# Reordering the prologue and the attention pace of a fused sparse-attention and softplus-MLP kernel

## The chip, the core and the metric

The kernel runs on one core of a Trainium2 chip. The metric is device time in microseconds of one execution; lower is better. A core has a matrix engine (TensorE, PE in the profile, with its weight loads listed as PEld), a vector engine (DVE), a scalar engine (ACT), GpSimd (POOL) and a queue processor that issues transfers (SyncE, SP). Matrix products land in PSUM; everything else on chip lives in SBUF.

## The reference

For 8 batches of 8 heads, 576 positions and head width 64, attention is computed with a mask: a position sees others at most 32 away, and 8 global positions see all and are seen by all. The result, 4608 tokens of width 512, goes through a two-layer product with a softplus between.

```python
scores = scale * np.matmul(q, k.transpose(0, 1, 3, 2))
mask = np.abs(pos[:, None] - pos[None, :]) <= window        # window = 32
mask = mask | is_global[:, None] | is_global[None, :]
scores = np.where(mask, scores, -1000000000.0)
attn = softmax(scores)
x = np.matmul(attn, v)                                       # heads side by side: 4608 x 512
h = x @ w_in                                                 # 512 x 2048
g = np.maximum(h, 0.0) + np.log1p(np.exp(-np.abs(h)))
out = g @ w_out                                              # 2048 x 512
```

## The kernel before

The work has two parts that share the engines: attention, batch by batch and in each batch by four pairs of heads, and the two-layer product, in 9 tiles of 512 tokens. Batch b fills columns 576b to 576b + 575 of `xT`, and tile n reads columns 512n to 512n + 511 of it, so tile 0 needs batch 0, tile 1 also batch 1, tile 2 also batch 2 and so on.

A pair of heads goes through these steps. `transposes` turns K and Q around on PE (line 258) into PSUM and copies them out to `KT` and `QT` (269, 271); the columns of the 8 global positions come from a one-hot product (263) in batches 0 and 1 and from `glob_T` through POOL copies (274 to 277) in later ones. `scores` multiplies them (291) and takes the exponential on ACT (299). `mask` multiplies with 0 or 1 on DVE (304). `sums` and `values` (325) multiply the result with ones and with V; `inv_ln` and `inv_exp` (344, 348) form the reciprocal of the sums on ACT; `scale_x` (357, 359) writes `xT` on DVE. `glob_sums` (335, 337) and `glob_norm` (365, 367) collect the rows of the global positions, and `glob_out` writes them into `xT` with 8 POOL copies (372).

A tile has 16 steps. In each, `mm1` makes one of 16 slices of the hidden layer (400: four 512-column matmuls into `hp`, then two ACT instructions, 403 and 404), and `mm2` does four of the 64 matmuls of the second product for the tile before (414); every fourth step ends with a copy of `o` (418) and a store. In tile 0 there is no `mm2`.

The order of the whole is written out by hand, and each engine runs its instructions in that order. Batch 0 is a prologue without tiles; its exponentials go into the buffer `first_ex`, and its global values come from a one-hot product (`value_globals`, 248). From then on `plan` holds, for each step and each of its two halves (after `mm1`, after `mm2`), the attention work to be done there. Times in the plan are counted in halves below: half 32 is the start of tile 1. `START` sets where batches 1 to 3 begin (steps 3, 20, 30, one pair each two steps); later batches have a pair each four steps, so that 16 steps hold a batch. `LOAD` and `CAST` set the step of a batch's loads and of its casts to bf16 on POOL.

Transfers of q, k, v and of the outputs are issued by SP in order (`load_runs` line 92, `load_v` 96). The weights are issued by POOL, cast on the way (`load_w_in` 424, `load_w_out` 428). The rows of K, Q and V at the global positions are gathered to a buffer in DRAM by `gather` (105) with 8 transfers per tensor, read back by `load_v_rows` (100) and by `load_global_columns` (380), cast (384) and transposed (388) into `glob_T`.

`warm` (502) runs matmuls on a constant tile whose result nobody reads. PSUM has in the prologue three two-bank regions for scores and value products (`region`) and two banks for transposes; later two regions, one transpose bank, two for `hp`, one for `o`.

Of the kernel before, what the change touches and what calls it, by code (L numbers as in the profile page):

```python
# [19 lines left out]
P = 128  # L20
# [20 lines left out]
def kernel(  # L41
# [42 lines left out]
    glob_T = {n: const.tile([P, NP, B * NG], BF16, name=f"{n}_gT") for n in "kq"}  # L84
    src = {"k": k, "q": q, "v": v}
    grow = {n: nc.dram_tensor(f"{n}_global_rows", (NG, B * HD), FP32, kind="Internal").ap() for n in "kqv"}
# [12 lines left out]
    def load_v_rows(b):  # L99
        nc.sync.dma_start(out=v_f[KW:P], in_=grow["v"][:, b * HD:(b + 1) * HD].unsqueeze(1).to_broadcast([NG, NTL, HD]))  # L100

    def gather(n, eng, first=0):
        sv = src[n].rearrange("b h s d -> (b h) s d")[first * H:]
        for g in range(NG):
            eng.dma_start(out=grow[n][g:g + 1, first * HD:].rearrange("o (c d) -> c o d", d=D),  # L105
                          in_=sv[:, bass.ds(regs[eng][g], 1), :])
# [22 lines left out]
    for p in range(2):  # L129
        load_runs("k", 0, [p])  # L130
        load_runs("q", 0, [p])
# [52 lines left out]
    load_v(0, half_heads[0])  # L184
    for p in range(2, NP):
        for n in "kq":
            load_runs(n, 0, [p])
    load_v(0, half_heads[1])
# [33 lines left out]
    masks = [const.tile([P, GW[i]], BF16, name=f"mask{i}") for i in range(2)]  # L222

    def scaled(eng, o, i, a, u=None):
        if eng is nc.scalar:
            eng.activation(out=o, in_=i, func=ACTF.Identity, scale=a, bias=0.0 if u is None else u)
        elif u is None:
            eng.tensor_scalar(out=o, in0=i, scalar1=a, scalar2=None, op0=ALU.mult)
        else:
            eng.tensor_scalar(out=o, in0=i, scalar1=a, scalar2=u, op0=ALU.mult, op1=ALU.add)  # L230

    def build_masks(tiles, eng):
        for t in tiles:
            m = masks[0 if t in GRP[0] else 1]
            c0 = GOFF[t] - (WLO[t] - (128 * t - 40))
            a, vl, n = akey[:, t:t + 1], vld[:, t:t + 1], ST[t]
            if t > 0:
                scaled(eng, m[:, c0:c0 + 40], band[:, 0:40], a)
            scaled(eng, m[:, c0 + 40:c0 + 40 + n], band[:, 40:40 + n], a, ukey[:])
            scaled(eng, m[:, c0 + 40 + n:c0 + 48 + n], band[:, 160:168], vl)  # L240
            if t < 4:
                scaled(eng, m[:, c0 + 168:c0 + 200], band[:, 168:200], a)
# [10 lines left out]
    def transposes(n, b, p, copy=nc.vector.tensor_copy):  # L253
        dst, rows = KT if n == "k" else QT, kqb[n, b]
        ps = psum["pool"].tile([P, 512], FP32, tag="tp", bufs=2 if b == 0 else 1, name="tp")
        tb = ps[:].bitcast(BF16)
        for r in range(RUN):
            nc.tensor.transpose(out=tb[:, r * NQ:(r + 1) * NQ], in_=rows[:, r, p * P:(p + 1) * P],  # L258
                                identity=ident_bf[:NQ, :NQ])
# [5 lines left out]
        else:  # L265
            copy = nc.vector.tensor_copy
            g = glob_T[n][:, p].rearrange("p (g b) -> p b g", b=B)[:, b]
# [17 lines left out]
    def scores(b, p, grp):  # L285
        sc = region(b, "sc")[:].rearrange("p (e c) -> p e c", e=2)
        for t in GRP[grp]:
            w = WHI[t] - WLO[t]
            for e in range(2):
# [3 lines left out]
                                 start=True, stop=True)  # L293
        if b == 0:
# [6 lines left out]

    def mask(p, grp):
        ex = exps[p, grp]
        nc.vector.tensor_tensor(out=ex, in0=ex, in1=masks[grp][:].unsqueeze(1).to_broadcast([P, 2, GW[grp]]),  # L304
# [10 lines left out]
    def over_keys(b, p, z, weights):  # L315
        av = AV[p, z] = region(b, "av")
        passes = [(slice(0, P), weights)]
        if b == 0 and not z:
            passes.append((slice(96, P), lambda t, e: VG[96:P, p * P + 64 * e:p * P + 64 * e + 64]))
        for j, (rows, weight) in enumerate(passes):  # L320
            for i, (t, lo, hi) in enumerate(PARTS):
                grp = 0 if t in GRP[0] else 1
                c = GOFF[t] + lo - WLO[t]
                for e in range(2):
                    nc.tensor.matmul(out=av[64 * e:64 * e + 64, OFF + lo:OFF + hi], lhsT=weight(t, e),  # L325
                                     rhs=exps[p, grp][rows, e, c:c + hi - lo],
                                     start=(j == 0 and lo in (0, SPLIT)),
                                     stop=(j == len(passes) - 1 and (i == len(PARTS) - 1 or hi == SPLIT)),
                                     skip_group_check=True, tile_position=(rows.start, 64 * e))
# [9 lines left out]
    def sums(b, p):  # L339
        over_keys(b, p, 1, lambda t, e: ones[:])  # L340
# [9 lines left out]
    def values(b, p):  # L350
        over_keys(b, p, 0, lambda t, e: V1[b % 2][:, t, p * P + 64 * e:p * P + 64 * e + 64])

    def scale_x(b, p):
# [5 lines left out]
        nc.vector.tensor_tensor(out=x[:, 480:576], in0=av[:, OFF + 512:OFF + 608], in1=rz[:, 512:608], op=ALU.mult)  # L359

# [14 lines left out]
    grows = {}  # L375

    def load_global_columns():
        for n in "kq":
            grows[n] = work.tile([B * NG, HD], FP32, tag=f"ex{0 if n == 'k' else 1}", bufs=2, name=f"{n}_rows")
            nc.sync.dma_start(out=grows[n][:], in_=grow[n].rearrange("g (b c) -> (g b) c", b=B))  # L380
# [232 lines left out]
```

## Time and profile before

| | us |
|---|---|
| median of 6 runs (386.74 to 388.4) | 387.56 |
| the profiled execution | 387.89 |
| its span, first to last instruction | 386.3 |
| PE busy | 347.3 (90%) |
| ACT busy | 275.4 (71%) |
| DVE busy | 182.6 (47%) |
| POOL busy | 119.2 (31%) |
| mean granted PE clock | 0.951 |
| moved by DMA | 43.64 MB, mean 113 GB/s |
| first `mm1` of tile 0 starts | 38.26 |
| first `mm1` of tile 1 starts | 74.94 |
| last `o` copy of tile 1 starts (step 15 of tile 2) | 164.85 |

Busy time is the time in which an engine has an instruction in work; for PE it also counts matmuls that run at a lowered clock, so it must be read together with the granted clock. A wait is written as the engine and line that waited, an arrow, and who released it, with the sum in us, the number of waits and the longest. A timeline has start, length, engine and line, the operation, output from inputs, the count, and in brackets the idle time before it with its releaser. The DMA share is the mean over 16 engines and can pass 1 where transfers overlap.

### The profile page before, as it was taken

The numbers are of one execution on the slowest core, as the hardware profiler recorded it, in microseconds if no ns is written. First come the engines' busy times: TensorE is split into PE (matmuls) and PEld (weight loads), VectorE is DVE, ScalarE is ACT, GpSimd is POOL, SyncE is SP. The second block draws the span as 40 slices with busy tenths as digits, with TensorE's granted clock in tenths as the row PEclk, the third lists the DMA queues.
The fourth block names the chain that finished last, engine by engine and source line by source line (L and its number), as shares of the span: only waits on it lengthen the run. The fifth ranks groups of instructions, "written<-read, shape, count | busy, mean of one in ns | idle before, by whom it ended". The sixth has DMA issues, their size and how long they took to land.

```text
span 386.3 us, 7411 instructions
## 1 busy us (share of the span) xinstructions
PE 347.3 (90%) x2761; PEld 178.1 (46%) x2801; DVE 182.6 (47%) x485; ACT 275.4 (71%) x438; POOL 119.2 (31%) x275
## 2 busy tenths in 40 slices
PE   6787877788888889999999999999999999999984
PEld 3564443334444444555455545554554444444432
DVE  7664177323665664675557556655554210100111
ACT  4742699764887787888888888888888767676500
POOL 7861770557308324343062308220200100000000
PEclk9556899996999999999999999999999999999999
DMA  7999449989519704591559156800000010010111
GB/s 168 240 260 212 100 76 214 252 199 235 105 39 235 160 30 139 162 143 45 151 151 160 55 152 158 152 28 29 29 27 30 27 56 27 27 56 27 53 57 54
DMA packets 62495, 43.64 MB, mean 113 GB/s; under 512 B 40932, under 2 KB 57444, under 8 KB 62460
## 3 DMA queue, kind: packets, MB, share of 16 engines
q1 hardware_dynamic: 57836, 38.86, 42.2%
q0 software_dynamic: 4480, 4.31, 6.8%
q8 instruction: 22, 0.36, 0.4%
q14 instruction: 13, 0.11, 0.1%
q10 hardware_dynamic: 144, 0.01, 0.0%
HBM read 37.92 MB, written 9.81 MB: 124 GB/s over the span
## 4 chain that ended last, share of the span: by engine, by line
PE 59%; issue 12%; DMA 9%; DVE 5%; SPq 5%; POOL 5%; ACT 1%; another core or an unknown queue 1%; POOLq 0%; ACTq 0%
PE o L414 27%; PE hp L400 22%; PE av L325 4%; PE tp L258 3%; PE sc L291 2%; SPq L105 2%; DVE ex L304 2%; DMA q_f<-in_q_dram 2%; DMA v_f<-in_v_dram 2%; POOL V L122 2%; DMA q_global_rows<-in_q_dram 2%; SPq L96 2%; DMA q_rows<-q_global_rows 1%; DMA v_f<-v_global_rows 1%
## 5 line engine op out<-in xcount | busy, mean ns | idle before, releaser
L400 PE MATMUL hp<-xT,w_in_t 128*128 128x512 bf16 x548 | 147.5, 385 | 3.7 <-POOL xT L372 2.1
L414 PE MATMUL o<-w_out_t,gt 128*128 128x512 bf16 x565 | 145.3, 381 | 4.4 <-DVE ot L418 3.3
L403 ACT ACTIVATE e<-hp 128x512 f32<-128x512 f32 x144 | 86.0, 597 | 61.0 <-PE hp L400 58.0
L404 ACT ACTIVATE gt<-e 128x512 bf16<-128x512 f32 x144 | 90.6, 630 | 4.5
L414 PEld LDWEIGHTS <-gt 128*128 128x128 bf16 x576 | 54.1, 98 | 67.5 <-issue 8.3
L400 PEld LDWEIGHTS <-w_in_t 128*128 128x128 bf16 x576 | 53.1, 99 | 65.9 <-issue 9.8
L418 DVE COPY ot<-o 128x512 f32<-128x512 f32 x36 | 24.8, 690 | 83.2 <-PE o L414 78.0
L304 DVE TENSOR_TENSOR ex<-ex,mask 128x1008 bf16<-128x1008 bf16 (+1 forms) x56 | 44.1, 795 | 30.7 <-ACT ex L299 29.7
L372 POOL COPY xT<-xg 128x4 bf16 x64 | 12.9, 202 | 129.7 <-DVE xg L367 126.3
L299 ACT ACTIVATE ex<-sc 128x1008 bf16<-128x1008 f32 (+1 forms) x56 | 48.5, 916 | 1.9 <-PE sc L291 1.9
L122 POOL CAST V<-v_f 128x512 bf16<-128x512 f32 (+3 forms) x50 | 27.8, 594 | 42.0 <-DMA v_f<-v_global_rows 36.3
L291 PE MATMUL sc<-QT,KT 64*128 64x200 bf16 (+2 forms) x320 | 21.5, 257 | 13.6 <-DVE xT L359 6.4
L344 ACT ACTIVATE rz<-av 128x616 f32<-128x616 f32 x32 | 21.8, 680 | 15.9 <-PE av L325 15.3
L269 DVE COPY KT<-tp 128x480 bf16<-128x480 bf16 x32 | 20.9, 652 | 25.7 <-PE tp L258 17.3
L118 POOL CAST qb<-q_f 96x1024 bf16<-96x1024 f32 (+1 forms) x24 | 24.3, 1031 | 7.5 <-DMA q_f<-in_q_dram 7.3
L118 POOL CAST kb<-k_f 96x1024 bf16<-96x1024 f32 (+1 forms) x24 | 24.5, 1044 | 3.9 <-PE sc L291 2.2
L335 DVE TENSOR_REDUCE gs<-av 128x8 f32<-128x32 f32 x64 | 11.9, 186 | 28.7 <-ACT rz L344 23.8
L357 DVE TENSOR_TENSOR xT<-av,rz 128x480 bf16<-128x480 f32 x32 | 20.9, 654 | 9.3 <-ACT rz L348 9.1
L291 PEld LDWEIGHTS <-KT 64*128 64x128 bf16 x320 | 12.2, 99 | 27.6 <-issue 11.2
L269 DVE COPY QT<-tp 128x480 bf16<-128x480 bf16 x28 | 18.4, 657 | 11.3 <-PE tp L258 10.2
L348 ACT ACTIVATE rz<-rz 128x616 f32<-128x616 f32 x32 | 22.7, 710 | 0.4
L325 PE MATMUL av<-ex,ones 128*64 128x160 bf16 (+1 forms) x336 | 18.6, 237 | 4.0 <-DVE ex L304 3.8
(102 smaller groups left out, 241.9 us busy)
## 6 DMA issues: line engine op xcount, KB each, us to landing
k_f<-in_k_dram SPq DMA_DIRECT2D x32, 288.0 KB, 5.6
q_f<-in_q_dram SPq DMA_DIRECT2D x32, 288.0 KB, 5.5
out_dram<-ot SPq DMA_DIRECT2D x36, 256.0 KB, 2.0
v_f<-in_v_dram SPq DMA_DIRECT2D x28, 240.0 KB, 5.5
w_in_t<-in_moe_w_in_dram POOLq DMA_DIRECT2D x4, 512.0 KB, 13.8
w_out_t<-in_moe_w_out_dram POOLq DMA_DIRECT2D x4, 512.0 KB, 10.3
v_f<-in_v_dram SPq DMA_DIRECT2D x7, 192.0 KB, 6.1
v_f<-in_v_dram SPq DMA_DIRECT2D x8, 120.0 KB, 6.7
```

What stands on the lines that cost most here:

```text
L118: eng.tensor_copy(o, i)
L122: eng.tensor_copy(V1[b % 2][:rows, t, cols], v_f[:rows, t, cols])
L269: copy(dst[:, p, 0:4, 0:KW].rearrange("p t (q r) -> p t q r", r=RUN), spread[:, 0:4 * NQT].rearrange("p (t q) r -> p t q r", q=NQT))
L291: nc.tensor.matmul(out=sc[:, e, GOFF[t]:GOFF[t] + w], lhsT=KT[r, p, t, :], rhs=QT[r, p].rearrange("p t c -> p (t c)")[:, WLO[t]:WHI[t]], s ...
L299: nc.scalar.activation(out=ex, in_=sc[:, :, 0:GW[grp]], func=ACTF.Exp, scale=SCALE)
L304: nc.vector.tensor_tensor(out=ex, in0=ex, in1=masks[grp][:].unsqueeze(1).to_broadcast([P, 2, GW[grp]]), op=ALU.mult)
L325: nc.tensor.matmul(out=av[64 * e:64 * e + 64, OFF + lo:OFF + hi], lhsT=weight(t, e), rhs=exps[p, grp][rows, e, c:c + hi - lo], start=(j == ...
L400: nc.tensor.matmul(out=hp[:], lhsT=w_in_t[:, kd, kf * P:(kf + 1) * P], rhs=xT[:, kd, n * NT:(n + 1) * NT], start=(kd == 0), stop=(kd == KD ...
L403: nc.scalar.activation(out=e[:], in_=hp[:], func=ACTF.Exp)
L404: nc.scalar.activation(out=gts[n][:, kf, :], in_=e[:], func=ACTF.Ln, bias=1.0)
L414: nc.tensor.matmul(out=op[:], lhsT=gts[n][:, kf, i * P:(i + 1) * P], rhs=w_out_t[:, kf, :], start=(kf == 0), stop=(kf == KF - 1))
L418: nc.vector.tensor_copy(ot[:], op[:])
```

## The change

In the prologue, all runs of K and Q of batch 0 are loaded ahead of V. The mask is built in 9 wide instructions on POOL and DVE instead of 18 narrow ones on POOL, ACT and DVE. Unread matmuls are put between the prologue's own: ahead of transposes and sums, a block of six after the first pair, and 14 instead of 4 at its end. The value products of a pair come one pair later for pair 0, and `scores` is split so that products and exponentials can stand apart. The gather of V's global rows is placed ahead of `glob_out(0)` on POOL and leaves out batch 0; the gathers of K and Q leave out batches 0 and 1. Chunks 2 and 3 of `w_in` are issued after `glob_out(0)` and the casts of batch 1, `w_out` at step 0 instead of 5; K and Q of batch 2 are loaded before the gathers on SP. The global columns are cast at step 12 and transposed at 13 and 14 instead of 15, in the buffer of `first_ex`. `PACE` replaces `START`: per batch the first half, the halves per pair, and the offsets of scores, sums, inverse and scaling. Batch 1 keeps its pace; batch 2 has 6 halves per pair from half 33 on, where it had 4 from 40 on; batch 3 has 7 from 55 on, where it had 4 from 60 on; later batches keep theirs, with `glob_norm` and `glob_out` two halves earlier.

```diff
+    FIRST = {"v": 1, "k": 2, "q": 2}
+    GB = B - FIRST["k"]
...
-    for p in range(2):
+    for p in range(NP):
         load_runs("k", 0, [p])
         load_runs("q", 0, [p])
...
-    load_v(0, half_heads[0])
-    for p in range(2, NP):
-        for n in "kq":
-            load_runs(n, 0, [p])
-    load_v(0, half_heads[1])
+    for h in range(2):
+        load_v(0, half_heads[h])
...
+    def build_mask_0(eng):
+        m = masks[0][:, 0:400].rearrange("p (t c) -> p t c", c=200)
+        times(eng, m[:, :, 0:160], slice(40, 200), slice(0, 2), 2)
...
-    def transposes(n, b, p, copy=nc.vector.tensor_copy):
+    def transposes(n, b, p, copy=nc.vector.tensor_copy, unread=0):
...
+        for _ in range(unread):
+            nc.tensor.matmul(out=ps[:], lhsT=junk[:, 0:P], rhs=junk[:], start=True, stop=True)
...
+        for _ in range(unread):
+            nc.tensor.matmul(out=av[:, 0:OFF], lhsT=junk[:, 0:P], rhs=junk[:, 0:OFF], start=True, stop=True,
+                             skip_group_check=True)
...
+    def head_values(b, p):
+        values(b, p)
+        values_of_globals(b, p)
+        glob_sums(b, p, 0)
+        scale_x(b, p)
...
+    def cast_global_columns():
+        nc.vector.tensor_copy(rows_b[:, 4:6], rows_f[:, 0:2])
...
-    LOAD = {2: (5, 6, 7), 3: (20, 20, 20), 4: (30, 30, 31)}
-    CAST = {2: 16, 3: 26}
-    START = {1: 3, 2: 20, 3: 30}
+    LOAD = {2: (None, None, 5), 3: (17, 18, 19)}
+    CAST = {2: 11, 3: 23}
+    PACE = {1: (6, 4, 2, 4, 5, 5), 2: (33, 6, 3, 6, 7, 8), 3: (55, 7, 4, 7, 8, 9)}
...
-        at(5, 0, load_w_out, c)
-    for n in "kq":
-        at(15, 1, lambda n: global_columns(n), n)
+        at(0, 0, load_w_out, c)
+    at(12, 0, cast_global_columns)
+    for i, n in enumerate("kq"):
+        at(13 + i, 1, global_columns, i, n)
...
+        start, pair, to_scores, to_sums, to_inverse, to_x = PACE.get(b, (2 * g0 - 13, 8, 4, 8, 9, 10))
...
+    for c in range(2):
+        load_w_in(c)
     load_positions(nc.gpsimd, mybir.EngineType.Pool)
-    scores(0, 0, 0)
-    scores(0, 0, 1)
+    for grp in range(2):
+        products(0, 0, grp)
+    exponentials(0, 0, 0)
     for p in range(NP + 1):
...
+        if p + 1 < NP:
+            transposes("k", 0, p + 1, unread=2)
+        if p == 0:
+            transposes("q", 0, 1, act_copy, unread=1)
+            exponentials(0, 0, 1)
+            cold = region(0, "cold")
+            for _ in range(6):
+                nc.tensor.matmul(out=cold[:, 0:512], lhsT=junk[:, 0:P], rhs=junk[:], start=True, stop=True)
...
-            sums(0, p - 1)
+            sums(0, p - 1, unread=3 if p < 3 else 0)
             inv_ln(0, p - 1)
-        if p + 1 < NP:
-            transposes("q", 0, p + 1, act_copy)
+        if p and p + 1 < NP:
+            transposes("q", 0, p + 1, act_copy, unread=2 if p == 1 else 1)
+        if p in (2, 3):
+            value_globals(half_cols[p - 2])
+        if p == 2:
+            head_values(0, 0)
...
+    gather("v", nc.gpsimd)
     glob_norm(0)
     glob_out(0)
     load_v(1)
-    gather("v", nc.gpsimd, 1)
     load_v_rows(1)
+    for i in range(2, NP):
+        for m in "kq":
+            cast_runs(m, 1, pair_heads(i), ALL, nc.gpsimd)
+    for c in range(2, 4):
+        load_w_in(c)
+    for n in "kq":
+        load_runs(n, 2)
     load_positions(nc.sync, mybir.EngineType.SP)
     for n in "kq":
         gather(n, nc.sync)
     load_global_columns()
-    warm(4)
+    warm(14)
```

## The prediction

> **What bounds the kernel now.** I read the slices first, then a table of stages cut at the tile borders, then the waits inside each stage. In the slices every digit is a tenth; PEclk is the granted TensorE clock.
>
> ```profile
> PE   6787877788888889999999999999999999999984
> PEclk9556899996999999999999999999999999999999
> DMA  7999449989519704591559156800000010010111
> ```
>
> From slice 16 on PE stands at 9 with the clock at 9 (full). Before that it has 6 to 8, the clock is at 5 in slices 2 and 3 and dips again in slice 10, and the DMA row is full except for a hole in slices 5 and 6. So the late part is PE's own work and the first 165 us are not. The stages (columns: window, length, busy us of PE, PEld, DVE, ACT, POOL, clock, DMA share, GB/s) are prologue, tile 0 (first product plus attention of batch 1), tiles 1 and 2, tiles 3 to 6, the rest:
>
> ```profile
> 0.00:38.26 38.26, 27.97 (x304) 18.72 (x306) 24.27 (x83) 18.86 (x38) 24.02 (x55) 0.64 1.06 220
> 38.26:74.94 36.68, 27.84 (x300) 14.88 (x304) 19.37 (x65) 30.70 (x48) 17.92 (x36) 0.95 0.80 157
> 74.94:164.85 89.91, 79.71 (x677) 40.94 (x688) 48.52 (x124) 65.32 (x100) 39.30 (x85) 0.96 0.63 146
> 164.85:308.90 144.05, 142.14 (x1176) 72.52 (x1190) 81.44 (x201) 120.85 (x189) 37.94 (x101) 1.00 0.39 90
> 308.90:386.30 77.40, 69.67 (x313) 31.08 (x318) 8.97 (x13) 39.62 (x65) 0.00 (x0) 1.00 0.12 45
> ```
>
> Tiles 3 to 6 are PE-bound (142.14 of 144.05). A finer cut shows the clock:
>
> ```profile
> 8.80:35.50 26.70, 21.82 (x268) 16.02 (x266) 17.30 (x52) 14.88 (x28) 15.75 (x23) 0.50 1.17 240
> 35.50:43.40 7.90, 5.76 (x19) 2.08 (x17) 0.52 (x3) 3.23 (x6) 6.01 (x17) 0.76 0.99 186
> 87.50:93.60 6.10, 5.62 (x36) 3.07 (x38) 1.90 (x4) 2.83 (x4) 4.80 (x16) 0.50 1.07 252
> ```
>
> From 8.8 to 35.5 us PE runs at half clock and is "busy" 82% of it, while no other engine passes 65%: the slow PE is the prologue's bound. The second dip starts with a data wait. These are POOL's timeline (start, length, idle before and its releaser), then PE's waits in tiles 1 and 2 and in tile 0:
>
> ```profile
> 36.12 2.09 POOL L372 COPY xT<-xg 128x4 bf16 x8 [9.79 <-DVE xg L367]
> 38.67 4.57 POOL L105 DMA_DIRECT2D v_global_rows<-in_v_dram  x8 [0.46 <-issue]
> 84.73 2.83 POOL L122 CAST V<-v_f 128x512 bf16<-128x512 f32 x5 [4.10 <-DMA v_f<-v_global_rows]
> ```
> ```profile
> PE sc L291 <- DVE xT L359: 4.2, 6, 0.7
> PE sc L291 <- POOL QT L276: 3.1, 2, 2.6
> ```
> ```profile
> PE tp L388 <- DVE k_rows_bf L384: 1.2, 1, 1.2
> PE tp L388 <- DVE q_rows_bf L384: 0.9, 1, 0.9
> ```
>
> V of batch 2 landed late, POOL sat in front of its cast 4.10 us, the K/Q copies queued behind it came late and PE stood 2.6 us, after which its clock was 0.50 for 6 us.
>
> [...] a group of four 512-column matmuls takes 1.89 us at 89 us and 1.03 us at 98 us (0.42 against 0.22 us apiece), and dense L400 work from 38.3 restored the clock at 42.7. [...] q0 and q1 together stay at 212 to 260 GB/s in slices 3 to 4[...].
>
> **The change, part by part.** The sum is over the profiled execution: 387.89 us, span 386.30 plus 1.59. The median of the runs is 387.56, 0.33 below.
>
> *Prologue, now 38.26.* Added on PE ahead of the first product: 10 unread 512-column matmuls inside the transposes, 6 as a block, 6 of 224 columns, 10 more at the end. The 16 and the 6 are 16 x 0.22 + 6 x 0.10 = 4.1 us at full clock, 16 x 0.42 + 6 x 0.19 = 7.9 at half. Up to the first scores (8.67) PE's work is the same, so I expect the same fall at 8.8. Then PE streams: scores 0.94, two unread 0.85, transposes 1.0, one 0.42, transposes 1.0, six 2.5: scores of pair 1 at about 15.3 (now 11.86). [...] From there ACT sets the pace. Per pair it does QT copies 0.98, Exp 1.74, Ln 0.68, Exp 0.75 = 4.15 us. Exp of pair 1 ends at 17.0, of pair 3 at 25.3. Then follow Ln and Exp of pair 2 (1.4), mask and sums of pair 3 beside these, its Ln and Exp (1.4), scale 0.9, normalization 0.5 and waits of some 1.3: xg at 30.8 (now 36.06). L372 takes 2.09, the start 0.5: first product at **33.5**. Ends: 29 if the clock is back by 12 us, 37 if ACT and DVE interleave badly.
> Covered: the value gather (8 issues, 4.57 us) moves ahead of L372 into POOL's 9.79 us of idleness; were POOL 6 us later, it would push the first product. The masks lose 4 ACT, 7 DVE (1.8 us) and 7 POOL (3.6) instructions and get 3 DVE and 6 POOL ones; these wide forms do not occur in the trace, the same elements bound them to between 1 us less and 1 us more, and ACT and DVE have room: 0. All K/Q runs go ahead of V on SP (ten V issues take about 10 us there, eight K/Q about 4): V's casts come some 3 us later, needed only at the third pass, which hides them. The first w_in chunk is issued after V's casts, about 21 us instead of 17.1; at 11.7 to 17.8 us to land that is 33 to 39: it may cost 0 to 4, taken in the range.
>
> *Tile 0, now 36.68.* Here ACT bounds (30.70 busy). Batch 1's pace is the same, half-steps and all. With the clock up, the first products save about 1.6 (16 in 5.30 us against 3.5 at full clock, partly held by ACT). The global columns, now at the end with 1.2 + 0.9 of PE waits and ACT's 1.9 us hole, move to steps 12 to 14 and save 2.4. Against it: w_in 2 and 3 (two issues, 1.5 us) are now behind L372 and four casts of batch 1 (3.3 us), at 37 to 38, and needed at steps 8 and 12, about 51 and 62; chunk 2 lands between 49 and 55. On SP eight K/Q loads of batch 2 (some 4 us of issue) now precede the 16 gathers (5.43 us per 8) and both row loads, so the rows land at 62 to 66 where step 12 wants them at 62. The new DVE cast waits for them, and behind it in DVE's queue stand the normalization of batch 1, thus POOL's L372, thus the first product of tile 1. I take +1.3 for both: **34.0**, ends 31 and 38. w_out is issued at about 42 (now 52.3), into the DMA hole: 0.
>
> *Tiles 1 and 2, now 89.91.* PE's floor: 64 groups x 0.873 (6.985 us per four tile steps without attention, from 308.89 to 315.87) = 55.9, plus 9.3 pairs x 2.05 (9.03 with attention less 6.985) = 19.0: 75. So 15 are lost: 3.1 and the half clock after it (some 3), 4.2 behind scaling, the rest where batches 2 and 3 run at a pair per two steps. That is PE 5.54 and ACT 2 x 1.23 + 3.2 = 5.66 at once, and the pairs came 6.5 apart. After, batch 2 takes three steps per pair: PE 7.29, ACT 6.9; batch 3 three and a half: 8.16 and 7.5. PE is the bound again. K/Q of batch 2 are there early. Scaling to next scores is still one half-step apart in batch 2 (3 x 0.7), two in batch 3 (0). V of batch 2 is still late in SP's queue, behind gathers and rows, and POOL's casts and L372 stand before the K/Q copies: 2. Together 75.4 + 4.1 = **79.5**, ends 77 and 86. Tiles 3 on keep pace and content: 221.4.
>
> Sum: 33.5 + 34.0 + 79.5 + 221.4 = 368.4, plus 1.59 less 0.33: **369.7**.
>
> **The rivals.** *The clock does not come back.* [...] then these cost 7.9 us on a PE that is the bound. First product at about 44, the rest as above: 380. For it: 26 us at half clock with PE 82% busy. Against: dense L400 needed only 4 us. *Data late.* DMA is at 1.17 already from 8.8 to 35.5; w_in 2, rows and V of batch 2 miss their steps by 3 us in tile 0 and 6 in tile 1, with one more clock dip: 379. For it: the 4.10 us in front of the V cast; against: the DMA hole of slices 5 and 6, some 10 us of transfer, gets filled. *Slower:* one mechanism, the rows of global columns. DVE's cast at step 12 is in order ahead of everything; if the 16 gathers, behind batch 2's runs and beside w_out, land so late that the rows come after about 81 us instead of 62 to 66, the wait eats all gains; at 87 the time is 394. Before, gathers issued at 46 to 58 gave rows at 68.9, which speaks against it. *Nothing of this:* unread matmuls on a prologue that data or ACT bounds anyway and paces that only move waits, no change; ACT's 14.88 us busy in 26.7 speaks against it.
>
> **How the numbers follow.** Forecast 0.55 (its own range 363 to 376); everything early (prologue 29, tile 0 at 31.5, tiles 1 and 2 at 77.5: 361) 0.10; clock 0.12; data late 0.12; slower 0.08; nothing 0.03. A measurement of this kernel can tell about 0.3% from no change. Range 361 to 381: it leaves out the slow case and the outer edges of the early and the late ones, under 2 in 10. Faster 0.88, same 0.03, slower 0.09.
>
> **What would show it.** Clock at 1.0 from about 15 us on and in the first product; POOL's L398 (now L372) at 31 us; tile 1's first product at 65 to 70; no PE wait over 2 us near the K/Q copies; o copies of tile 2's end near 147. I am wrong if the clock stays at 0.5 past 20 us, if DVE's global cast waits over 5 us, or if pairs of batch 2 come closer to 9 than 8 us apart.

## The result, and the profile after

The changed kernel takes 384.47 us (median of 16 runs, 381.83 to 386.57); the kernel before took 387.48 in the same comparison (37 runs). The ratio is 0.9924, with a 95% interval of 0.9904 to 0.9944: faster by 3.0 us (0.8%), where 17.9 were forecast (387.56 to 369.7) and the range ended at 381. The profiled execution took 386.18, span 384.6, so its sums stand 1.7 above the median. One execution in this document, the 380.61 us of e12_vlater, was in a slower state than the rest of its run: it counts in that run's median below, which is 376.82 without it, and not in its ratio.

The slices of the changed kernel (page, one digit for each 9.6 us: PE busy, granted PE clock, DMA):

```profile
PE   7864867788978899999999999999999999999984
PEclk9998889999999999999999999999999999999998
DMA  7999899886733905580569156900000010010111
```

The clock is at 9 in the first three slices, where it had been 5 in slices 2 and 3. (The trace has no clock record ahead of 7.19 us, and a stretch without one counts as full in the page; up to 5.89 us PE's unread 512-column matmuls start 0.43 us apart, against 0.42 apiece at half clock and 0.22 at full in the kernel before.) But PE's own row has a 4 in slice 4, just ahead of the first product, and the clock dips to 8 in slices 4 to 6 (cut by the microsecond it is 0.50 from 28 to 31, from 38 to 41 and from 52 to 55 us). The stages, cut at the same events as before (window, length, busy us of PE, PEld, DVE, ACT, POOL, clock, DMA share, GB/s):

```profile
0.00:38.53 38.53, 26.75 (x334) 16.38 (x338) 24.27 (x79) 17.80 (x34) 26.98 (x61) 0.95 0.98 211
38.53:76.73 38.20, 28.57 (x299) 15.55 (x304) 21.15 (x65) 29.62 (x47) 14.54 (x31) 0.92 1.02 196
76.73:163.16 86.43, 76.42 (x675) 39.52 (x687) 48.96 (x124) 66.00 (x102) 39.21 (x84) 1.00 0.56 134
163.16:307.20 144.04, 141.79 (x1176) 72.42 (x1189) 78.97 (x201) 120.82 (x189) 38.77 (x101) 1.00 0.39 90
307.20:384.60 77.40, 69.67 (x313) 31.01 (x318) 8.98 (x13) 39.63 (x65) 0.00 (x0) 0.99 0.11 44
```

The span fell by 1.7: prologue +0.3, tile 0 +1.5, tiles 1 and 2 -3.5, the rest 0. Against the forecast the prologue is 5.0 too long (38.53 against 33.5), tile 0 4.2 (38.20 against 34.0), tiles 1 and 2 6.9 (86.43 against 79.5). These add up to the whole error of the span, 16.2.

Where the prologue's gain went is in two timelines of the changed kernel, DVE's and POOL's (start, length, idle before and its releaser):

```profile
31.66 0.19 DVE L393 TENSOR_TENSOR xg<-gs 128x32 bf16<-128x32 f32 x1
```
```profile
27.02 1.67 POOL L109 DMA_DIRECT2D v_global_rows<-in_v_dram  x3 [0.20 <-issue]
32.50 0.52 POOL L109 DMA_DIRECT2D v_global_rows<-in_v_dram  x1 [3.81 <-DMA w_in_t<-in_moe_w_in_dram]
35.91 0.52 POOL L109 DMA_DIRECT2D v_global_rows<-in_v_dram  x1 [2.90 <-DMA w_in_t<-in_moe_w_in_dram]
36.43 2.05 POOL L398 COPY xT<-xg 128x4 bf16 x8
```

`xg` was ready at 31.85, as forecast within 1.1 (before: 36.06). The scatter that turns it into `xT` (L398) started 4.6 later, behind the seventh and eighth value gathers. Each of these stood for the landing of a `w_in` chunk, with which it has no data in common. The semaphores of the instructions in the trace show why: POOL's transfers signal on eight completion counters in turn, 111 to 118. The queue is w_in 0 (111), w_in 1 (112), then eight gathers (113 to 118 and again 111 and 112), and the last two, the ninth and tenth transfers, carry a wait on 111 and 112. The last signal of w_in 0 came at 32.21 and that of w_in 1 at 35.63, 0.3 us ahead of each issue.

PE's waits in tile 0 of the changed kernel (waiter, releaser, sum, count, longest), and DVE's and POOL's timelines around its longest mask wait:

```profile
PE av L342 <- DVE ex L320: 4.9, 7, 2.2
PE hp L428 <- POOL xT L398: 4.8, 1, 4.8
```
```profile
48.58 3.26 DVE L320 TENSOR_TENSOR ex<-ex,mask 128x1008 bf16<-128x1008 bf16 x2 [2.08 <-ACT ex L311]
57.67 1.30 DVE L320 TENSOR_TENSOR ex<-ex,mask 128x1008 bf16<-128x1008 bf16 x2 [1.56 <-ACT ex L311]
```
```profile
49.35 2.06 POOL L122 CAST kb<-k_f 96x1024 bf16<-96x1024 f32 x2
```

PE idled 4.8 us ahead of the first product, its clock was half again at 38 to 41, and the 16 products took 4.97 us (5.30 before). The two masks of a pair take 1.30 us at 57.67 and 3.26 at 48.58, where POOL casts K of batch 2 at the same time. PE waited 2.2 for them, and ran at 0.50 from 52 to 55.

### The profile page after: what moved, and what is told of

Same layout as the page of the kernel before. It is cut to its first block, busy times and chain, and to the rows that moved or that the text cites. A ratio compares the mean times of both kernels' runs of the same rounds, so it can differ in the third digit from the quotient of the medians.

```text
span 384.6 us, 7461 instructions
## 1 busy us (share of the span) xinstructions
PE 343.2 (89%) x2792; PEld 174.9 (45%) x2833; DVE 182.3 (47%) x480; ACT 273.9 (71%) x434; POOL 119.5 (31%) x274
## 4 chain that ended last, share of the span: by engine, by line
PE 66%; issue 11%; DVE 6%; ACT 5%; POOL 5%; DMA 3%; SPq 2%; another core or an unknown queue 1%; POOLq 0%; ACTq 0%; DVEq 0%
PE o L442 28%; PE hp L428 27%; PE av L342 5%; PE tp L265 3%; PE sc L300 3%; ACT ex L311 2%; DVE ex L320 2%; DVE ot L446 2%; DMA q_f<-in_q_dram 1%; POOL V L126 1%; DMA v_f<-in_v_dram 1%; POOL qb L122 1%; ACT e L431 1%; SPq L99 1%
## 5 line engine op out<-in xcount | busy, mean ns | idle before, releaser
L398 POOL COPY xT<-xg 128x4 bf16 x64 | 15.7, 245 | 128.1 <-DVE xg L393 124.7
L126 POOL CAST V<-v_f 128x512 bf16<-128x512 f32 (+3 forms) x50 | 26.1, 564 | 39.2 <-DMA v_f<-v_global_rows 33.8
L300 PE MATMUL sc<-QT,KT 64*128 64x200 bf16 (+2 forms) x320 | 19.2, 240 | 8.3 <-DVE xT L379 3.3
L342 PE MATMUL av<-ex,ones 128*64 128x160 bf16 (+1 forms) x336 | 17.9, 235 | 7.0 <-DVE ex L320 6.7
L122 POOL CAST kb<-k_f 96x1024 bf16<-96x1024 f32 (+1 forms) x24 | 23.2, 993 | 0.3 <-DMA k_f<-in_k_dram 0.3
L300 PEld LDWEIGHTS <-KT 64*128 64x128 bf16 x320 | 10.8, 94 | 22.3 <-issue 12.2
```

The lines of the kernel that those rows point to most:

```text
L122: eng.tensor_copy(o, i)
L126: eng.tensor_copy(V1[b % 2][:rows, t, cols], v_f[:rows, t, cols])
L300: nc.tensor.matmul(out=sc[:, e, GOFF[t]:GOFF[t] + w], lhsT=KT[r, p, t, :], rhs=QT[r, p].rearrange("p t c -> p (t c)")[:, WLO[t]:WHI[t]], s ...
```

## The experiments

Each run was compared with runs of the kernel before on the same chip (medians 387.2 to 387.7). "First product" is the first `mm1` of tile 0, "scatter 1" the start of `glob_out(1)`, 2.0 to 2.3 ahead of tile 1's first product (4.0 in the kernel before, where the global columns came last), "end" the start of the last `o` copy of tile 1; these three columns come from one profiled execution, which can lie 2.5 us off the median. After "end" the span had 221.4 us to go in each of them.

| run | first product | scatter 1 | end | median us | ratio to before (95%) |
|---|---|---|---|---|---|
| before | 38.26 | 70.96 | 164.85 | 387.5 | |
| after | 38.53 | 74.64 | 163.16 | 384.47 | 0.9924 (0.9904 to 0.9944) |
| e1_split | 33.09 | 70.83 | 160.63 | 382.91 | 0.9899 (0.9862 to 0.9936) |
| e2_late | 38.49 | 71.73 | 162.10 | 385.27 | 0.9946 (0.9929 to 0.9964) |
| e3_border | 38.36 | 74.67 | 159.82 | 380.36 | 0.9822 (0.9784 to 0.9859) |
| e5_nounread | 38.76 | 75.53 | 163.03 | 385.16 | 0.9941 (0.9923 to 0.9958) |
| e6_two | 36.21 | 69.90 | 160.19 | 380.97 | 0.9828 (0.9801 to 0.9855) |
| e7_two56 | 36.73 | 69.33 | 154.39 | 378.84 | 0.9776 (0.9748 to 0.9804) |
| e8_two_nounread | 36.05 | 70.26 | 158.61 | 381.98 | 0.9850 (0.9820 to 0.9879) |
| e9_two56early | 37.69 | 70.76 | 158.87 | 380.70 | 0.9809 (0.9774 to 0.9843) |
| e10_gathercasts | 35.33 | 69.28 | 156.69 | 378.21 | 0.9754 (0.9713 to 0.9794) |
| e11_oldpace | 38.14 | 71.67 | 173.82 | 398.29 | 1.0271 (1.0228 to 1.0315) |
| e12_vlater | 36.53 | 70.71 | 154.75 | 377.29 | 0.9710 (0.9667 to 0.9753) |
| e13_oldpace20 | 38.16 | 70.51 | 159.75 | 383.59 | 0.9915 (0.9884 to 0.9947) |
| e14_behind | 35.33 | 69.39 | 155.68 | 376.90 | 0.9723 (0.9692 to 0.9753) |

### The gather in front of the scatter

Two runs take the wait away by order alone. The first puts the two waiting gathers behind the scatter (`gather` gets a third argument, the positions that it takes; this line of its definition is left out in the excerpts below):

```diff
-    gather("v", nc.gpsimd)
+    gather("v", nc.gpsimd, range(6))
     glob_norm(0)
     glob_out(0)
+    gather("v", nc.gpsimd, range(6, NG))
```

> The changed kernel, but only six of the eight value gathers stand ahead of glob_out(0) on POOL, the last two behind it. Theory A (a gather reuses the semaphore of a w_in chunk issued eight transfers earlier and POOL stands until that chunk has landed, so glob_out(0) comes 4.6 us after xg): glob_out(0) starts at 32 us instead of 36.4, the first product at 34.3 instead of 38.5 with the clock at 1.0, and the time falls by 4 to 7 us against the changed kernel, to 378 to 380.5. Theory B (the first product waits for w_in chunk 0, which lands at 32.5, or for DMA in general): glob_out(0) comes early, but the first product stays near 38 and the time within 1 us of the changed kernel.

The second puts two gathers ahead of the weights, so that the seventh and eighth re-use the counters of gathers:

```diff
+    load_positions(nc.gpsimd, mybir.EngineType.Pool)
+    gather("v", nc.gpsimd, range(2))
     for c in range(2):
         load_w_in(c)
-    load_positions(nc.gpsimd, mybir.EngineType.Pool)
...
-    gather("v", nc.gpsimd)
+    gather("v", nc.gpsimd, range(2, NG))
```

> Two of the eight value gathers go ahead of the first two w_in chunks in POOL's queue, the other six stay; nothing else changes. Theory A (gathers 7 and 8 wait because they re-use the completion counters of w_in chunks 0 and 1): now the 7th and 8th gather re-use the counters of two gathers, so no gather waits for w_in any more; the POOL scatter L398 of batch 0 starts right after the gathers or xg, about 32 to 33 us, the first product at 33.5 to 35 (w_in 1.2 us later at most), its 16 products in about 4 us. The V rows are written some 5 us earlier than in the run with two gathers behind the scatter, so V of batch 1 is cast by about 40 us without a wait. Tile 1's first product at 71.5 to 73, last copy of tile 1 near 160, time 379.5 to 382.5. Rival (the gain is given back later whatever the gather does, because tile 0 has its own limits: data of batch 1 and ACT): first product early as above, but tile 1's first product at 75 or later and the time 383.5 to 385.

POOL's timeline of the run with two gathers behind, and PE's:

```profile
30.99 2.04 POOL L398 COPY xT<-xg 128x4 bf16 x8 [2.36 <-DVE xg L393]
35.09 0.52 POOL L109 DMA_DIRECT2D v_global_rows<-in_v_dram  x1 [1.15 <-DMA w_in_t<-in_moe_w_in_dram]
45.67 3.51 POOL L126 CAST V<-v_f 128x256 bf16<-128x256 f32 x10 [5.45 <-DMA v_f<-v_global_rows]
```
```profile
33.09 3.88 PE L428 MATMUL hp<-xT,w_in_t 128*128 128x512 bf16 x16 [0.95 <-POOL xT L398]
46.12 1.72 PE L342 MATMUL av<-ex,V 128*64 128x160 bf16 x12 [2.29 <-POOL V L126]
```

The first product comes at 33.09 (33.5 was forecast), at full clock. But the rows of V come late in turn, PE stands 2.29 for them and falls to half clock (four 512-column matmuls take 1.87 us at 48.43 and 1.89 at 51.13, against 1.03 at full clock), and of the 5.4 us only 1.6 is left in the time, with intervals that overlap; theory A's 378 to 380.5 was missed. With two gathers ahead no gather waits, and the V cast only 1.07 (POOL's timeline of e6_two):

```profile
27.29 3.14 POOL L109 DMA_DIRECT2D v_global_rows<-in_v_dram  x6
33.79 2.04 POOL L398 COPY xT<-xg 128x4 bf16 x8 [3.36 <-DVE xg L393]
41.43 3.50 POOL L126 CAST V<-v_f 128x256 bf16<-128x256 f32 x10 [1.07 <-DMA v_f<-v_global_rows]
```

The time is 380.97, 3.5 below the changed kernel, the same amount of work in another order. The re-use of counters is thereby shown as the cause of the late scatter, and the time agrees with theory A (379.5 to 382.5) and not with its rival. The first product came 1.2 to 2.7 later than that theory said, mainly since `xg` came at 33.54; what stands behind that follows in the next two groups.

### What the unread matmuls are worth

All unread matmuls inside the prologue are left out and 4 of the 14 at its end kept, once in the changed kernel and once with two gathers ahead:

```diff
-            cold = region(0, "cold")
-            for _ in range(6):
-                nc.tensor.matmul(out=cold[:, 0:512], lhsT=junk[:, 0:P], rhs=junk[:], start=True, stop=True)
...
-    warm(14)
+    warm(4)
```

> The changed kernel without its unread matmuls in the prologue (none between transposes and sums, no block of six, 4 instead of 14 at the end). Theory G (they hold the clock, and the clock shortened the prologue to xg at 31.7): the clock falls to 0.5 near 9 us, xg comes at 35 to 37; glob_out(0) then waits hardly longer than it does for the gather now (36.4), so the first product comes at 38 to 39.5 and the time is within 1.5 us of the changed kernel: their gain is hidden behind the gather. Rival H (they hold the clock and that carries into the tiles): 4 us or more slower.

> Two gathers ahead of w_in, and all unread matmuls inside the prologue left out (no result depends on them), 4 instead of 14 behind it. With the gather's wait gone the clock is all that differs: xg 1.5 us later than with the unread matmuls (33.2 against 31.7, as measured with the gather's wait in place). Theory G (the unread matmuls are worth the 1.5 us of xg plus the first products at full clock, 1.3 us): first product 2.5 us or less later than in the first run of this call, time 1.5 to 3 us longer than it. Rival (xg's lead is lost in POOL's queue, which has the gathers in front of the scatter anyway): within 0.7 us of it.

The clock row of the page without them (changed kernel otherwise):

```profile
PEclk9555789999999999999999999999999999999999
```

The prologue is back at half clock, yet `xg` comes at 33.18 (35 to 37 were expected), only 1.5 after 31.66, and the time is 385.16 against 384.47: no difference that the intervals tell apart. From before to after `xg` moved by 4.2, so the larger part of that comes from the prologue's other reordering, which no run takes apart further. Even the 1.5 is one execution against one: in the five runs that keep the changed kernel's prologue as it is (after, e2_late, e3_border, e11_oldpace, e13_oldpace20) `xg` starts at 30.43 to 32.34. What was ahead at `xg` was lost in POOL's queue. With the gather's wait gone the difference is 1.0 (381.98 against 380.97); the intervals overlap, and the result lies between the two expectations, so the worth of the unread matmuls stays open, somewhere from 0 to 2 us.

Three things in the traces stand against them. They did not hold the clock to the end of the prologue: in the changed kernel it was half from 27.67 to 31.08 us, and its mean over the prologue was 0.95 there and in e3_border, 0.91 in e7_two56 and 0.87 in e13_oldpace20. In e6_two `xg` came at 33.54, hardly ahead of the 33.71 without them. DVE's masks of pair 3 took 3.27 us in e6_two (next group) and 1.34 in e8_two_nounread. And the block of 14 at the prologue's end stands ahead of the first product in PE's own order. PE's timeline of e7_two56 (next but one group), where the scatter ended at 35.67:

```profile
31.85 4.62 PE L527 MATMUL cold<-w_out_t 128*128 128x512 bf16 x14
36.73 3.88 PE L428 MATMUL hp<-xT,w_in_t 128*128 128x512 bf16 x16 [0.26 <-PE cold L527]
```

In the six runs that have both the two gathers ahead and this block, it held the first product back by 0.3 to 1.1 us. A shorter block alone was not tried.

### Masks on DVE while POOL casts

The change had moved the K/Q casts of batch 2 from step 16 of the plan to step 11. Here they go to step 12, behind the scatter of batch 1 in POOL's queue (a second line, left out here, keeps the V casts at their steps):

```diff
-    CAST = {2: 11, 3: 23}
+    CAST = {2: 12, 3: 23}
```

> The changed kernel, with all K and Q casts of batch 2 behind glob_out(1) on POOL (CAST of batch 2 at 12 instead of 11; its V casts keep their steps). Theory C (the two K casts that POOL runs at 49.4 to 51.4 slow the masks of the first pair of batch 1 on DVE from 1.3 to 3.3 us, and PE loses 2.2 us of waiting and 2 us at half clock): that mask pair takes 1.3 to 1.6 us, PE does not wait for it and keeps its clock, tile 0 is 3 to 4 us shorter; then the two casts come 2 us later in front of the K/Q copies of batch 2, so the total gains 1 to 3 us. Rival D (the masks are slow because of transfers or of what DVE itself does): the masks still take over 2.5 us and the time is the same or 1 to 2 us longer.

DVE's timeline of this run, same place as 48.58 above:

```profile
48.87 1.30 DVE L320 TENSOR_TENSOR ex<-ex,mask 128x1008 bf16<-128x1008 bf16 x2 [2.08 <-ACT ex L311]
```

The masks are back at 1.30, scatter 1 comes at 71.73 instead of 74.64. So the casts stretched the masks, as theory C said. Its gain of 1 to 3 us did not come, the time is the same (385.27): the casts now stand behind the scatter, and at the start of batch 2 PE waits for them (1.2 and 0.7) and for the K copies as before (2.0). A cast at step 11 of the plan had run beside the mask of step 4, because POOL had nothing else in its queue and the data lay there.

The kernel before had such pairs too, and they could have been read before the forecast. DVE's and POOL's timelines of it:

```profile
157.19 2.87 DVE L304 TENSOR_TENSOR ex<-ex,mask 128x1008 bf16<-128x1008 bf16 x2 [0.68 <-ACT ex L299]
```
```profile
156.18 3.44 POOL L118 CAST kb<-k_f 96x1024 bf16<-96x1024 f32 x3 [2.24 <-PE sc L291]
```

I compared every mask instruction of these two traces with the casts beside it. The 103 that overlap no K/Q cast have a median of 0.68 us. The 23 that overlap one by more than 0.3 us have a median of 1.40, from 0.58 to 3.02; one of them took under 0.75. By itself that describes and proves nothing; e2_late is the proof. Why the two disturb each other no run here shows.

Three further runs moved the same casts about. In all, two gathers are ahead and batch 3 starts at half 56 (378.84, next group). First, all six K/Q casts of batch 2 at step 11:

```diff
-                    at(c0 + (3 * i + c) // 2, 0, cast_runs, n, b, every, slice(2 * c, 2 * c + 2), nc.gpsimd)
+                    at(11 if b == 2 else c0 + (3 * i + c) // 2, 0, cast_runs, n, b, every, slice(2 * c, 2 * c + 2), nc.gpsimd)
```

> As the second run of this call, and all six K/Q casts of batch 2 stand at step 11, ahead of the scatter of batch 1 in POOL's queue, instead of two per step from 11 to 13. Theory (what PE loses at the start of batch 2, 2.3 us to the KT copies, the half clock after it and 1.1 us to the Q copies, comes from casts queued behind the scatter): the K/Q copies of batch 2 come early, tile 1's last copy another 1 to 2 us earlier, time 374.5 to 377.5. Rival (more POOL casts beside the DVE masks of batch 1 stretch more of them from 1.3 to 3.3 us per pair of masks): tile 1's first product 1 to 2 us later, time 0 to 1.5 us longer than the second run.

Measured 380.70. PE did not gain at the start of batch 2: the QT copies were late there by 3.6 instead of 2.0, behind V casts that had waited 5.69 for V's rows, and a mask pair of batch 1 took 2.48. Scatter 1 came 1.4 later and the median is 1.9 up, with intervals that overlap: nearer to the rival, and no gain. Then, again from 378.84, the six late gathers ahead of the four K/Q casts of batch 1:

```diff
+    gather("v", nc.gpsimd, range(2, NG))
     for i in range(2):
         for m in "kq":
             cast_runs(m, 1, pair_heads(i), ALL, nc.gpsimd)
-    gather("v", nc.gpsimd, range(2, NG))
```

> Two gathers ahead of w_in and batch 3 from half-step 56 (378.84 us measured), and in POOL's queue the other six gathers now stand ahead of the four K/Q casts of batch 1, instead of behind them. In the run with two gathers ahead, the masks of pair 3 of batch 0 took 3.27 us for two instead of 1.3 to 1.7, at 24.50, while POOL ran these casts (23.70 to 27.3), and the reciprocal operand xg came at 33.54 instead of 30.7. Theory H (POOL's large strided casts and DVE's bf16 masks disturb each other): now the casts run from about 28 to 31.5, the masks at 24.5 take 1.3 to 1.7, xg at 31 to 31.7, first product at 33.5 to 34.5; time 375.5 to 378. Rival (the masks were late for another reason, DMA traffic of w_in and rows): masks stay at about 3 us, first product 36 to 37, time 378 to 380. The casts may push the scatter if POOL is not done by 31.5: then 1 us of the gain goes.

DVE's timelines without and with this edit (e6_two, which has the same prologue as e7_two56 without it, where the pair took 2.71; then e10_gathercasts):

```profile
24.50 3.27 DVE L320 TENSOR_TENSOR first_ex<-first_ex,mask 128x1008 bf16<-128x1008 bf16 x2
```
```profile
24.67 1.16 DVE L320 TENSOR_TENSOR first_ex<-first_ex,mask 128x1008 bf16<-128x1008 bf16 x2
31.59 1.16 DVE L393 TENSOR_TENSOR xg<-gs 128x32 bf16<-128x32 f32 x1
```

The masks are short again and the first product comes at 35.33 instead of 36.73, but the casts, now at 29.6 to 32.7, hit `xg` instead (1.16 us instead of 0.19). Theory H holds for the masks and not for the first product (33.5 to 34.5); 378.21 is not told apart from 378.84. Last, the casts behind the scatter, with the V edit of the next group:

```diff
-    for i in range(2):
-        for m in "kq":
-            cast_runs(m, 1, pair_heads(i), ALL, nc.gpsimd)
     gather("v", nc.gpsimd, range(2, NG))
     glob_norm(0)
     glob_out(0)
     load_v(1)
     load_v_rows(1)
+    for i in range(2):
+        for m in "kq":
+            cast_runs(m, 1, pair_heads(i), ALL, nc.gpsimd)
```

> All that helped, together: two gathers ahead of w_in, batch 3 from half-step 56, V of batch 2 cast two steps later (377.29 us measured), and the four K/Q casts of batch 1 moved behind the scatter of batch 0, so that POOL runs none of them while DVE does the masks and xg of batch 0 (they stretched one mask pair to 3.27 and xg to 1.16 us). Theory H: masks at 24.5 take 1.2 to 1.7, xg at 31 to 31.7 in 0.19 us, scatter right after it, first product at 34 to 34.6; time 374 to 377. Rival (what the earlier start gains is lost at the global rows, for which DVE's cast already waited 1.57 us and PE 2.4 us at 69.5): first product as early, tile 1 begins no earlier than 71, time 377 to 378.5.

376.90, within theory H's time but not told apart from 377.29 without the edit; tile 1 began at 71.49, as the rival said. `xg` took 0.19 again, at 32.54, but the last gathers waited 4.00 for earlier gathers' counters, and the disturbance moved to batch 2. POOL's and DVE's timelines of e14_behind:

```profile
79.49 3.00 POOL L122 CAST kb<-k_f 96x1024 bf16<-96x1024 f32 x3
```
```profile
79.61 3.91 DVE L320 TENSOR_TENSOR ex<-ex,mask 128x1008 bf16<-128x1008 bf16 x2 [3.10 <-ACT ex L311]
```

### The pace of batches 2 and 3

In the changed kernel the first pair of batch 3 starts at half 55, one after batch 2's last scores, and its own scores fall on half 59, the one in which batch 2's last pair is scaled. One number shifts it:

```diff
-    PACE = {1: (6, 4, 2, 4, 5, 5), 2: (33, 6, 3, 6, 7, 8), 3: (55, 7, 4, 7, 8, 9)}
+    PACE = {1: (6, 4, 2, 4, 5, 5), 2: (33, 6, 3, 6, 7, 8), 3: (56, 7, 4, 7, 8, 9)}
```

> The changed kernel, with batch 3 starting one half-step later (56 instead of 55). Theory E (at the border of batches 2 and 3 the scores of the new batch stand in the same half-step as the scaling of the old one and its transposes right behind the old scores, so PE waits 1.65 us for a K copy and 1.66 us for an exponential at 113 and 119 us): both waits go below 0.8 and the time falls by 2 to 3 us. Rival F (ACT's and DVE's total work sets the pace there): the waits move to the next pairs and the time stays within 0.7 us.

> As the run before, and batch 3 starts at half-step 56 instead of 55. If the gain of the gather order (5 us at the first product, by theory A 2 to 5 at the end) and of the border between batches 2 and 3 (3.3 us at the end of tile 1's copies, measured alone) add up: 376 to 379, tile 1's last copy near 157. If they are two views of one slack (an earlier tile 1 meets batch 3's data late): 379 to 381.

PE's waits in tiles 1 and 2, the changed kernel and then e3_border:

```profile
PE tp L265 <- DVE KT L278: 2.0, 2, 1.6
PE sc L300 <- ACT ex L311: 1.7, 1, 1.7
```
```profile
PE sc L300 <- DVE xT L379: 2.3, 4, 0.8
PE sc L300 <- POOL QT L283: 1.1, 1, 1.1
PE av L342 <- DVE ex L320: 1.0, 1, 1.0
```

The two waits of the border are gone, tiles 1 and 2 take 83.1 instead of 86.4, the time is 380.36: worth 4.1 us, more than all of the change and than the 2 to 3 of theory E. The same two waits stand in e1_split, e2_late and e6_two, and in no run that starts batch 3 at 56. With two gathers ahead the time is 378.84: of the two gains, 3.5 and 4.1, 5.6 is there together, within the 376 to 379 expected of a sum, though 2.0 short of it.

What PE waits for next, 2.0 for the QT copies of batch 2, comes from V casts in front of them in POOL's queue:

```diff
-                at(c0 + (4 if b == 2 else 3) + t // 3, 0, cast_v, b, t, nc.gpsimd)
+                at(c0 + (6 if b == 2 else 3) + t // 3, 0, cast_v, b, t, nc.gpsimd)
```

> Two gathers ahead of w_in and batch 3 from half-step 56 (378.84 us measured), and POOL's casts of V of batch 2 two steps later, at steps 17 and 18 instead of 15 and 16, so behind the K/Q global-column copies of pair 0. In that run these copies waited behind the V casts (0.81 for the rows and 2.83 of casts at 76.08 to 78.85), PE stood 2.0 for POOL's QT copy at 79.1. Theory (the V cast in front of the copies is the wait at the start of batch 2): POOL's QT copies come right after the qb casts at 75.3, the 2.0 of PE goes, time 376 to 378.3. Rival (what comes next is just as late: qb casts or V itself at the first value products): PE waits 1.5 to 2.5 in another place between 76 and 86, time 378 to 379.5.

377.29: the QT wait is gone from the trace. In tile 0 of this run DVE's cast of the global columns waits 1.57 for its rows and PE 2.4. The median moved by 1.5, into the theory's range, and the interval (0.9667 to 0.9753) just overlaps that of the run without the edit.

Last, the old steps of batches 2 and 3 in the changed kernel, once with a load misplaced and once right:

```diff
-    LOAD = {2: (None, None, 5), 3: (17, 18, 19)}
-    CAST = {2: 11, 3: 23}
+    LOAD = {2: (None, None, 5), 3: (20, 20, 20)}
+    CAST = {2: 16, 3: 26}
...
-    PACE = {1: (6, 4, 2, 4, 5, 5), 2: (33, 6, 3, 6, 7, 8), 3: (55, 7, 4, 7, 8, 9)}
+    PACE = {1: (6, 4, 2, 4, 5, 5), 2: (40, 4, 2, 4, 5, 5), 3: (60, 4, 2, 4, 5, 5)}
...
-                at(c0 + (4 if b == 2 else 3) + t // 3, 0, cast_v, b, t, nc.gpsimd)
+                at(c0 + 3 + t // 3, 0, cast_v, b, t, nc.gpsimd)
```

> The changed kernel with the steps of batches 2 and 3 and of their K/Q casts put back to those of the kernel before (start 40 and 60 half-steps, a pair every 4, casts from step 16 and 26); the reordered prologue, the earlier loads and the batch 1 steps stay. Theory C (the wider paces are worth most of what tiles 1 and 2 gained, 3.5 us, and cost 2 us in tile 0 through casts beside masks): tile 0 is 2 us shorter than 38.2 (masks of batch 1 at 1.3 us a pair), tiles 1 and 2 take 89 to 91 as before, time 385.5 to 388. Rival (the paces are worth nothing, the gain comes from batch 2's K/Q lying ready early): tiles 1 and 2 near 86, time 382 to 384.5.

> The run with the old steps of batches 2 and 3 was slow (398.29) because its load of batch 3's V stood one step ahead of the last two casts of batch 2's V, which so waited 13.79 us and took batch 3's data. Here that load is put back to step 20, where it is in the kernel before. So: the changed kernel, with old steps, casts and loads of batches 2 and 3. Theory C (the wider paces are worth the 3.5 us by which tiles 1 and 2 got shorter, less the 2 us that the early casts cost in tile 0): tile 0 about 36, tiles 1 and 2 89 to 91, time 385.5 to 388. Rival (the paces gave nothing, K/Q of batch 2 lying ready did): tiles 1 and 2 at 85 to 87, time 381.5 to 384.

The first, which left the `LOAD` line as it was, tells nothing of the pace: V's casts waited 13.79 us in it for batch 3's load, and its 398.29 is 13.8 above the changed kernel. The second is not told apart from the changed kernel. Its stages, as above:

```profile
0.00:38.16 38.16, 29.94 (x338) 17.47 (x338) 23.89 (x79) 17.79 (x34) 27.35 (x61) 0.87 1.02 214
38.16:72.60 34.44, 26.63 (x304) 14.32 (x304) 19.22 (x65) 29.50 (x47) 12.55 (x29) 1.00 1.01 200
72.60:159.75 87.15, 79.45 (x686) 39.88 (x687) 48.68 (x124) 66.23 (x102) 39.88 (x86) 0.98 0.61 139
```

Tile 0 takes 34.44, with masks of 1.30 and a full clock, and tiles 1 and 2 87.15. So between these two traces the wider paces won 0.7 us in tiles 1 and 2. That is not told apart from nothing: the runs with the changed kernel's paces (e1_split, e2_late, e5_nounread, e6_two, e8_two_nounread) take 85.4 to 88.3 there. The shorter tiles 1 and 2 (89.91 before) so come mostly from the rest of the change; that K/Q of batch 2 are loaded earlier by it is the likely part, but that alone was not tried. The casts that came with the paces lost 2.9 at scatter 1 (e2_late). The rival's time is met, and its 85 to 87 for tiles 1 and 2 but for 0.15.

## Why the prediction was wrong, point by point

- **The clock in the prologue: up for most of it, as forecast, but worth little.** It was full from 7.2 to 27.7 us, where I had expected a fall to half at 8.8 and, as an estimate of mine, a return at 15, and was half from there to 31, after PE had stood 1.89 us for DVE's copy of VG. `xg` came at 31.66 (30.8 forecast) and at 30.73 in e1_split. But I had read "the slow PE is the prologue's bound" from a PE that was 82% busy at half clock, and e5_nounread, at half clock in slices 2 to 4 (9.6 to 38.4 us), with its first 16 products in 5.47 us where full clock takes 3.88, still has `xg` at 33.18, 2.7 ahead of the kernel before. What I credited to the clock came mostly from the other reordering.
- **The gather "covered by POOL's 9.79 us of idleness": the step that failed first, 5.0 us.** I counted the issue time, 4.57, and asked what would happen if POOL were late. I did not ask what a gather itself waits for. I had put the start of the `w_in` chunks at 21 and their landing at 33 to 39; they were issued from 20.38 on and landed at 32.2 and 35.6, and the last two gathers waited for just that. Moving them away gives 33.09 (e1_split) and 3.5 us of time (e6_two).
- **Tile 0, 34.0: the terms hold when nothing collides.** e13_oldpace20 has 34.44. In the changed kernel 4.2 were lost: the first products at half clock again after the gather's wait (4.97 instead of 3.88 us), and the stretched masks with 2.2 of wait and the half clock after it. Neither was in my sum. I had the new casts' place in the plan, step 11, and not the time at which POOL would come to them, nor what a cast does to a mask beside it.
- **The rows of the global columns: not late in the changed kernel.** PE waited 0.7 there; I had taken 1.3 for it and the `w_in` chunks together. The slower rival did not occur. The wait appears once the rest is faster: 2.4 in e12_vlater.
- **Tiles 1 and 2, 79.5: the floor was right, the waits were mis-sized.** 75.4 (0.4 more than its own terms, 55.9 and 19.0, give) against 76.42 us of PE busy; 4.1 of waits against 10.0 without work. I took each batch's pace by itself and did not lay the last pair of batch 2 over the first of batch 3: 3.3 us (e3_border). The V casts in front of the K/Q copies I had, at 2; they were 1.1 to 3.6. Of the larger idea, that wider paces win most of ten us, at most 0.7 appears as the change has it, and 4.1 with the border moved (87.15 in e13_oldpace20, 83.1 in e3_border).
- **From the end of tile 2 on: right,** 221.4 forecast and 221.4 in every run.
- **The rivals:** by number "nothing of this", which I gave 0.03, was the nearest, 3.1 us off, and much of it holds: the unread matmuls gained little in a prologue that PE's clock bounded little, and the paces as first set gained 0.7 us at most. By its kind "data late" (379) came close, but w_in 0 and 1 were not among the transfers it named. "The clock does not come back" did not occur. None of them had POOL's queue, where the cause lay twice, first as a waiter and then as a neighbour of DVE.

The two best runs, e12_vlater and e14_behind, are not told apart. e14_behind is at 376.90 us, 2.0% under the changed kernel and 2.8% under the one before. Its profiled execution (span 377.1, 378.71 us, 1.8 above its median) is 8.7 over the forecast's 368.4: 1.8 at the first product (35.33 against 33.5), 2.2 in tile 0 (36.16 from there to tile 1's first product at 71.49, against 34.0) and 4.7 in tiles 1 and 2 (84.2 against 79.5), of which 2.2 is one wait of PE for a stretched mask pair. What the rest would need stays open.

## What to carry to other kernels

Ask of every moved transfer not only how long its issue takes but what it has to wait for, counters of earlier transfers on its queue included (3.81 and 2.90 us here); the cheapest mend is often another order of the same instructions. Casts that stood at step 11 of the plan ran at 49.35, as soon as POOL came to them, beside a mask pair that then took 3.26 us: look at what a moved instruction will run beside. Before crediting a gain to a slow engine, ask what else would still take as long. And lay the end of one batch over the start of the next before trusting a pace.

## What the runs showed of the hardware that was not expected

- POOL's transfers in this program signal on eight counters in turn, and in the changed kernel the seventh and eighth value gathers waited 3.81 and 2.90 us for the two `w_in` chunks eight places before them, whose data they do not use. Behind other transfers the last gathers waited 0 (e6_two) to 4.00 us (e14_behind).
- DVE's masks took longer beside POOL's K/Q casts: pairs of 3.26 and 3.50 (changed kernel), 3.27 (e6_two) and 3.91 us (e14_behind), where pairs with none beside took 1.30 (e2_late) and 1.16 (e10_gathercasts). `xg`, 0.19 us alone, took 1.16 beside a cast (e10_gathercasts).
- With unread matmuls among the transposes the changed kernel's prologue had a granted clock of 1.00 from 7.2 to 27.7 us in the profiled execution; without them (e5_nounread) it was 0.5 in slices 2 to 4 of the page. But the same prologue, at a mean of 0.95 in the changed kernel, had 0.87 in e13_oldpace20.
- In the changed kernel the clock fell to half within a wait of PE of 4.8 us (at 37.91) and within one of 2.2 between short bursts of work (at 51.56), for 3.41 us each. Behind a wait of 3.0 ahead of the first product, in e13_oldpace20, the 16 products took 3.88 us and the clock of the stage was 1.00.
- The stretches at half clock up to tile 2 lasted 3.41, 3.41 and 3.41 us in the changed kernel (from 27.67, 37.91 and 51.56) and 27.31, 3.41 and 6.83 in the kernel before (from 8.58, 39.30 and 87.09). Why equal prologues differ in their clock was not tested.
